# Larger row transfers limited by bytes, a shared phi load, logit blocks by bank pairs, and a moved head order in a convolution and soft-MoE kernel

## The chip, the cores and the metric

The kernel runs on 1 core of one Trainium2 chip. The metric is the device time of one execution in microseconds (us); of several runs the median is taken.

## What is computed

A causal convolution of 7 taps, whose weights are a softmax over the taps of each of 8 heads, is followed by a soft mixture of experts over all 28,672 rows. Everything is float32.

```
x: (8, 3584, 192)   weight: (8 heads, 7 taps)   phi: (192, 32)   w1: (8, 192, 1024)   w2: (8, 1024, 192)
w = softmax(weight, axis=-1)
y[b, s, head h] = sum_k w[h, k] * x[b, s - 6 + k, head h]          # 24 channels a head, zeros before row 0
y = y.reshape(28672, 192)
logits = y @ phi                                                   # (28672, 32 slots)
d = softmax(logits, axis=0); slot_input = d.T @ y                  # over all rows: needs the whole of y
slot_out[e] = relu(slot_input[e] @ w1[e]) @ w2[e]                  # 4 slots for each of 8 experts
out = softmax(logits, axis=1) @ slot_out                           # (28672, 192)
```

## The kernel before

The 8 sequences are 8 batches. A batch's x (2.75 MB) is held in SBUF as 32 windows of 128 rows (`xs`, two buffers in turn), its convolution as `xc` (two buffers), and the transposed convolution as `xt` (one buffer).

- **Loads** (`load_x(b)`): four groups of 8 windows, each in transfers of two windows (256 rows of 768 bytes, 192 KB), and two small transfers for the first window. All DMAs are issued by SyncE (SP), which takes them strictly in order. `load` lets a transfer go only when the one six before it has landed (`WINDOW = 6`). For each group GpSimd (POOL) then copies 6 halo rows (`L184`; for batch 0 in halves, on POOL or ScalarE). The transfers of batch b+2 overwrite `xs` of batch b, so they wait for the last convolution matmul of batch b.
- **Convolution** (`conv(b)`, `L422`): per head 8 matmuls against a banded matrix `toep`, into the PSUM buffers `cv0` and `cv1` in turn, copied to `xc` by ScalarE (ACT, `L182`) or VectorE (DVE, `L186`). Each head reads all of the batch's windows. Batch 0 goes by halves (`L466`). `toep` is built at the start in two halves of four heads, by small copies (`bput`).
- **Transposes** (`turns`, `L443`): six 32x32 block transposes by DVE, one for each block of 32 channels.
- **Logits** (`chain(b)`, `L508`): six blocks k of 32 matmuls, 16 into the bank pair `lg0` (a = 0, 1) and then 16 into `lg1` (a = 2, 3), which accumulate over k. Then a maximum of each bank pair (`fmax`, `L520`, DVE), the running maximum and its negative (`fmin`, `L532` and `L533`), the exponentials (`fexp`, `L539`, ACT, with the negative maximum as bias), eight transposes through the PE (`L554`), their copies, and 64 matmuls that sum the slots' inputs (`L570`), added up in `acc`.
- **The rows' softmax** (`rows(b)`, `L599` to `L619`): maximum, subtraction, exponential, sum and division over the 32 slots, on DVE, POOL and ACT, put into gaps of the schedule.
- **phi**: four DMAs (`L398`) put the same 24 KB on four groups of 32 partitions (`phi4`).
- **Experts and output**: w1 and w2 (12.6 MB) are loaded into gaps and into buffers that come free (`load_w`), the experts run after batch 7 (`L745` to `L799`), then `L828` makes the output, which SP stores (`L850`, `L858`).

The order of all this is written by a planner (`Plan`). Each step is added with a cost for each engine that may run it, what it reads and writes, and a priority (the lower goes first). `Plan.order` simulates the engines with these costs, a delay `LAG` between an engine's end and another's start, and a look-ahead `LOOK`, and emits the steps in the order of the simulated start. Every engine then runs its steps in that order, whatever the real times are. Steps of priority 1000 and above (weights, `rows`) are put into gaps that the first pass left.

Of the kernel before, what the change touches and what calls it, by code (L numbers as in the profile page):

```python
# [10 lines left out]
ALU = mybir.AluOpType  # L11
# [4 lines left out]
class Plan:  # L16
# [2 lines left out]


    ENG = ("PE", "ACT", "DVE", "POOL", "DMA")
    LAG = {"PE": 0.2, "ACT": 0.2, "DVE": 0.16, "POOL": 0.2, "DMA": 2.1}
    SELF = {"PE": 0.0, "ACT": 0.08, "DVE": 0.1, "POOL": 0.1, "DMA": 2.1}
    LOOK = {"PE": 0.05, "ACT": 0.3, "DVE": 0.2, "POOL": 0.0, "DMA": 0.0}
    SLIP = 0.05
# [5 lines left out]
    def add(self, fn, cost, reads=(), writes=(), prio=0.0, after=()):  # L31

        i = len(self.steps)
        deps = {self.writer[r] for r in reads if r in self.writer}
        for w in tuple(writes) + tuple(after):
            if w in self.writer:
                deps.add(self.writer[w])
            deps.update(self.readers.get(w, ()))
        for r in reads:
            self.readers.setdefault(r, []).append(i)  # L40
        for w in writes:
            self.writer[w] = i
            self.readers[w] = []
        deps.discard(i)
        self.steps.append((fn, cost, deps, prio))
# [95 lines left out]
def tile_conv_softmoe(ctx: ExitStack, tc: tile.TileContext, x, weight, phi, w1, w2, out):  # L141
# [12 lines left out]
    TB = T // 2  # L154
    NI = NW // 2
    U = 8
    NB = D // 32
    NQ = S // 4
    TQ = NQ // P
# [8 lines left out]
    def act(n):  # L168
        return 0.19 + n / 1200

    def dve(n):
        return 0.13 + n / 960
# [1 line left out]
    def pool(n):  # L174
        return 0.12 + n * 0.00217

    def dma(nbytes, rate=330e3):
        return {"DMA": nbytes / rate}

    def copy(e, dst, src):  # L180
# [53 lines left out]

    WINDOW = 6
    issued = []

    def load(dst, src):  # L240
        i = nc.sync.dma_start(dst, src).ins  # L241
        if len(issued) >= WINDOW:
            tc.add_manual_dep(
                i, issued[-WINDOW].name, mybir.DependencyInfo(mybir.DependencyClass.Sync, mybir.DependencyReason.DATA),
                reason="short queues",
            )
        issued.append(i)

# [4 lines left out]
    def load_x(b):  # L255
        s = b % 2
        xv = xs[s]
        base = b * S - PRE
        np_ = NW // 4

        def src(row0, rows, i0, n):
            return bass.AP(x.tensor, (base + 2 * T * i0 + row0) * D, ap=[[D, rows], [2 * T * D, n], [1, D]])

        for k in range(4):
            i0, i1 = k * np_, (k + 1) * np_

            def fn(e, k=k, i0=i0, i1=i1):
                if k == 0:

                    nc.sync.dma_start(xv[16:P, 0:1, :], src(16, P - 16, 0, 1))  # L270
                    nc.sync.dma_start(xv[PRE:16, 0:1, :], src(PRE, 16 - PRE, 0, 1))
                    i0 = 1
                if k == 3 and b == B - 1:

                    i1 -= 1
                    nc.sync.dma_start(xv[0:112, i1 : i1 + 1, :], src(0, 112, i1, 1))
                    nc.sync.dma_start(xv[112 : P - 2, i1 : i1 + 1, :], src(112, P - 2 - 112, i1, 1))
                for i in range(i0, i1, 2):
                    n = min(2, i1 - i)
                    load(xv[:, i : i + n, :], src(0, P, i, n))  # L280

            add(fn, dma(P * np_ * D * 4), reads=[f"z{s}"], writes=[xsk[s][k]] + [f"{xsk[s][k]}.{i}" for i in range(2)], prio=b * 10 - 30)

            im = (i0 + i1) // 2
            if b == 0:
                halves = (("POOL", "ACT"), i0, im), (("POOL", "ACT"), im, i1)
            else:
                halves = ((("POOL",), i0, i1),)
            for j, (es, a0, a1) in enumerate(halves):
                add(  # L290
                    lambda e, a0=a0, a1=a1: copy(e, xv[0:ZS, a0:a1, :], xv[64 : 64 + ZS, a0:a1, :]),
                    {en: 0.1 + (a1 - a0) * D * 0.0009 for en in es}, reads=[xsk[s][k]], writes=[f"{xsk[s][k]}.{j}"], prio=b * 10 - 30,
                )

    def load_w(parts, nbytes, key, after, prio):
        def fn(e):
            for dst, src in parts:
                load(dst, src)

        add(fn, dma(nbytes), reads=["begun"], writes=[key], after=after, prio=prio)  # L300

# [1 line left out]
    wv = wb.rearrange("p (h k) -> p h k", k=KT)  # L303
    add(
        lambda e: nc.sync.dma_start(wb, bass.AP(weight.tensor, 0, ap=[[0, P], [1, H * KT]])),
        {"DMA": 0.3}, writes=["wb"], prio=-100,
    )

    add(lambda e: nc.gpsimd.memset(xs[0][0:16, 0, :], 0.0), {"POOL": 0.25}, writes=["z0"], prio=-101)
# [32 lines left out]
    for i in range(2):  # L342
        h0, h1 = i * HG, (i + 1) * HG
        prod = fe[:, (H + h0 * KT) * BW : (H + h1 * KT) * BW].rearrange("p (h c k) -> p h c k", c=BW, k=KT)

        def bprod(e, prod=prod, h0=h0, h1=h1):
            w_ = wv[:, h0:h1, :].unsqueeze(2).broadcast_to((P, HG, BW, KT))
            sh = bass.AP(shf.tensor, shf.offset, ap=[shf.ap[0], [0, HG], [1, BW], [1, KT]])
            veng(e).tensor_tensor(out=prod, in0=sh, in1=w_, op=ALU.mult)

        def bsum(e, prod=prod, h0=h0, h1=h1):
            nc.vector.tensor_reduce(out=band[:, h0:h1, :], in_=prod, axis=AX.X, op=ALU.add)

        n = HG * BW * KT
        add(bprod, {"POOL": pool(n)} if i else {"DVE": dve(n)}, reads=["wb", "shf"], writes=[f"prod{i}", f"e0.{i}"], prio=-42 + i)
        add(bsum, {"DVE": dve(n)}, reads=[f"prod{i}"], writes=[f"band{i}"], prio=-40 + i)


        for a, (p0, rows, off, blks) in enumerate((
            (0, 32, -8 - ZS, (0,)), (0, 8, T - ZS, (1,)), (32, 32, 24 - ZS, (0, 1)),  # L360
            (64, 32, -ZS, (0, 1)), (96, 32, 32 - ZS, (0, 1)),
        )):
            for k in blks:
                t0, t1 = max(TB * k, off), min(TB * k + 32, off + BW)

                def bput(e, p0=p0, rows=rows, off=off, h0=h0, h1=h1, t0=t0, t1=t1, k=k):
                    sl = slice(p0, p0 + rows)
                    copy(e, toep[sl, h0:h1, t0 + (32 - TB) * k : t1 + (32 - TB) * k], band[sl, h0:h1, t0 - off : t1 - off])

                m = HG * (t1 - t0)  # L370
                add(
                    bput, {"ACT": act(m), "DVE": dve(m), "POOL": 0.15 + m * 0.0011}, reads=[f"band{i}", "tz"],
                    writes=[f"toep{i}.{a}.{k}"], prio=-40 + i,
                )
    toepk = [[f"toep{i}.{a}.{k}" for a, k in ((0, 0), (1, 1), (2, 0), (2, 1), (3, 0), (3, 1), (4, 0), (4, 1))] for i in range(2)]
# [18 lines left out]
        )  # L394

    def phi_load(e):
        for a in range(4):
            nc.sync.dma_start(phi4[32 * a : 32 * a + 32], phi.rearrange("(k p) n -> p k n", p=32))  # L398


    def selector(e):
        nc.vector.tensor_reduce(out=gsel[:, 0:NS], in_=ident.rearrange("p (g n) -> p n g", n=NS), axis=AX.X, op=ALU.add)
# [8 lines left out]
    def conv(b):  # L411
# [3 lines left out]
        for h in range(H):  # L415
# [15 lines left out]
                    cv[k][:, :, 0 : NI * CG].rearrange("p f (i c) -> p f i c", c=CG),  # L431
                )

            add(mm, {"PE": 0.72}, reads=all_(xk) + toepk[h // HG], writes=[f"cv{k}"], prio=pr)
            add(ev, {"ACT": act(2 * NI * CG), "DVE": dve(2 * NI * CG)}, reads=[f"cv{k}", "one"], writes=xck[s][h], prio=pr)

    def turns(b):
# [59 lines left out]
    def chain(b):  # L497
# [1 line left out]
        last = b == B - 1  # L499
        n = U * TB  # L500

        for k in range(NB):

            def lmm(e, k=k):
                for a in range(4):
                    r = slice(32 * a, 32 * a + 32)
                    for c in range(4):
                        nc.tensor.matmul(  # L508
                            lg[a // 2][32 * c : 32 * c + 32, a % 2, 0:n].rearrange("p (u j) -> p u j", j=TB),
                            phi4[r, k, :], xt[r, k, U * c : U * c + U, 0:TB],  # L510
                            start=(k == 0), stop=(k == NB - 1), tile_position=(32 * a, 32 * c),
                        )

            add(lmm, {"PE": 0.66}, reads=xtk[k] + ["phi4"], writes=["lg0", "lg1", "lmm"], prio=pr)

        el = eall[:, b].rearrange("p (g u k j) -> p g k u j", g=2, k=2, j=TB)
        for g in range(2):
# [11 lines left out]
        mx, old, nm = nmr[:, b + 1, 2:3], nmr[:, b, 2:3], nmr[:, b, 3:4]  # L529

        def fmin(e):
            nc.vector.tensor_reduce(out=mx, in_=nmr[:, b, 0 : 3 if b else 2], axis=AX.X, op=ALU.max)  # L532
            nc.vector.tensor_scalar(out=nm, in0=mx, scalar1=-1.0, scalar2=None, op0=ALU.mult)  # L533

        add(fmin, {"DVE": 0.2}, reads=[f"nr{b}.{g}" for g in range(2)] + [f"nm{b - 1}"], writes=[f"nm{b}"], prio=pr)
        for g in range(2):

            def fexp(e, g=g):
# [6 lines left out]
        if b:  # L545
            add(
                lambda e: nc.scalar.activation(al[b % 2], old, AF.Exp, bias=nm),
                {"ACT": 0.2}, reads=[f"nm{b}", f"nm{b - 1}"], writes=[f"al{b % 2}"], prio=pr + (0.5 if last else 0),
            )
        for v in range(2):  # L550

# [75 lines left out]
        add(turn, {"DVE": dve(n)}, writes=ks, prio=pr + 100)  # L627

    load_x(0)
    add(phi_load, {"DMA": 0.5}, reads=["xs0.3"], writes=["phi4"], prio=-25)  # L630
    load_x(1)
    conv_halves(0)
    for b in range(B):
# [40 lines left out]
    for i in range(8):  # L674
# [7 lines left out]

    add(
        lambda e: nc.tensor.matmul(cv[0][:, 0, 0:P], mxf.broadcast_to((P, P)), ident, start=True, stop=True),
        {"PE": 0.25}, reads=[f"nm{B - 1}", "ident"], writes=["cv0"], prio=75.5,
    )

    def merge(e):
# [202 lines left out]
```

## Time and profile before

| | |
|---|---|
| median of 3 runs | 227.83 us (226.12 to 228.55) |
| profiled execution | 230.08 us, of which the span from first to last instruction is 228.2 us |
| mean granted TensorE clock of that execution | 0.918 |
| read from HBM and written to it | 37.79 MB and 22.02 MB |

PE is TensorE, PEld its weight loads, SP SyncE's queue. A wait is named by what ended last before it. The profiled execution took 1.0% more than the median.

### The profile page before, as it was taken

Reading aid. Unit: us, or ns where it says so; the run is one execution under the profiler, and the core shown is the slowest. Engines: PE = TensorE matmul, PEld = TensorE weight load, DVE = VectorE, ACT = ScalarE, POOL = GpSimd, SP = SyncE. Lnnn points to the kernel's source line nnn. Section 1 sums busy time; section 2 is a strip of 40 time slices with the busy share of each in tenths; the row PEclk is TensorE's granted clock in tenths of the full one; section 3 lists DMA queues with packets and bytes.
Section 4 is the critical chain, followed back from the end, with each engine's and each line's share of the span. In section 5 each row is a group of like instructions: output and inputs, shape, how many; then the busy total and the mean of one; then the engine's idle time right before and its main releaser. Section 6 shows DMA issues by size and latency. Waiting matters only on the chain.

```text
span 228.2 us, 7982 instructions
## 1 busy us (share of the span) xinstructions
PE 181.1 (79%) x3410; PEld 112.5 (49%) x3410; DVE 155.1 (68%) x236; ACT 91.9 (40%) x140; POOL 100.5 (44%) x110
## 2 busy tenths in 40 slices
PE   4586469989969979999779999989989999776000
PEld 2164335325425525436325546655768899765000
DVE  5999318948759869899649999576277986544000
ACT  3465205456225156173065292322147755456000
POOL 5642556616633585725846624227755850000000
PEclk9999859999979999999979999999999999877555
DMA  4997988789969998486774698889109999999995
GB/s 124 276 283 203 313 253 262 266 254 284 294 196 272 282 266 264 117 247 197 230 201 123 153 206 236 269 280 302 47 28 359 375 404 411 411 413 406 415 417 236
DMA packets 49583, 60.33 MB, mean 264 GB/s; under 512 B 4606, under 2 KB 43404, under 8 KB 49548
## 3 DMA queue, kind: packets, MB, share of 16 engines
q1 hardware_dynamic: 49548, 59.82, 81.0%
q8 instruction: 27, 0.44, 0.8%
q14 instruction: 8, 0.07, 0.1%
HBM read 37.79 MB, written 22.02 MB: 262 GB/s over the span
## 4 chain that ended last, share of the span: by engine, by line
PE 37%; DMA 30%; SPq 8%; DVE 5%; issue 4%; ACT 4%; POOL 4%; DVEq 1%; ACTq 0%; POOLq 0%
DMA xs<-in_x_dram 26%; PE cv L422 10%; PE cv L828 8%; PE lg L570 6%; SPq L241 6%; DMA out_dram<-xt 4%; PE lg L508 2%; PE lg L785 2%; POOL eall L611 2%; PE lg L828 2%; PE lg L554 2%; ACT xs L182 2%; PE cv L745 2%; POOL xs L184 1%; PE cv L676 1%
## 5 line engine op out<-in xcount | busy, mean ns | idle before, releaser
L184 POOL COPY xs<-xs 6x1536 f32<-6x1536 f32 (+1 forms) x31 | 43.3, 1396 | 57.3 <-DMA xs<-in_x_dram 55.1
L422 PE MATMUL cv<-xs,toep 64*64 64x384 f32 x448 | 52.3, 540 | 12.1 <-POOL xs L184 6.3
L182 ACT COPY xc<-cv 128x768 f32<-128x768 f32 x40 | 32.4, 819 | 56.7 <-PE cv L422 53.9
L443 DVE STREAM_TRANSPOSE xt<-xc 128x1024 f32<-128x1024 f32 x42 | 49.1, 1215 | 1.3 <-ACT xc L182 1.3
L508 PE MATMUL lg<-xt,phi 32*32 32x224 f32 x1536 | 32.5, 361 | 4.0 <-issue 2.0
L422 PEld LDWEIGHTS cv<-xs,toep 64*64 64x64 f32 x448 | 16.3, 141 | 37.0 <-issue 11.6
L828 PE MATMUL cv<-so,eall 32*128 32x192 f32 x256 | 30.0, 457 | 4.6 <-ACT xs L182 2.1
L611 POOL TENSOR_TENSOR eall<-eall,rms 128x896 f32<-128x896 f32 x16 | 26.9, 1699 | 14.7 <-DVE rms L615 9.7
L508 PEld LDWEIGHTS lg<-xt,phi 32*32 32x32 f32 x1536 | 19.6, 103 | 19.3 <-issue 10.5
L828 PEld LDWEIGHTS cv<-so,eall 32*128 32x128 f32 x256 | 24.1, 314 | 8.2 <-ACT xs L182 3.3
L186 DVE COPY xc<-cv 128x768 f32<-128x768 f32 x20 | 18.9, 955 | 11.2 <-PE cv L422 10.7
L570 PE MATMUL lg<-xc,dn 128*32 128x193 f32 x512 | 22.8, 329 | 0.3 <-ACT dn L182 0.3
L828 PE MATMUL lg<-so,eall 32*128 32x192 f32 x192 | 22.2, 415 | 0.0
L828 PEld LDWEIGHTS lg<-so,eall 32*128 32x128 f32 x192 | 20.5, 323 | 0.4 <-DVE xs L186 0.2
L619 DVE STREAM_TRANSPOSE eall<-eall 128x896 f32<-128x896 f32 x16 | 17.5, 1099 | 4.0 <-POOL eall L611 4.0
L570 PEld LDWEIGHTS lg<-xc,dn 128*32 128x32 f32 x512 | 15.7, 110 | 8.7 <-ACT dn L182 4.7
L182 ACT COPY xs<-cv 128x768 f32<-128x768 f32 x14 | 11.1, 800 | 16.2 <-PE cv L828 13.8
L539 ACT ACTIVATE dT<-lg,nmr 128x448 f32<-128x448 f32 x16 | 9.3, 632 | 13.4 <-DVE nmr L533 13.3
L602 POOL TENSOR_TENSOR tree<-eall 128x448 f32<-128x448 f32 x8 | 9.2, 1153 | 11.1 <-ACT eall L623 10.9
L186 DVE COPY xs<-cv 128x768 f32<-128x768 f32 x10 | 9.4, 952 | 5.8 <-PE lg L828 2.9
L520 DVE TENSOR_SCALAR_CACHE_REDUCE eall<-lg 128x448 f32<-128x448 f32 x16 | 9.3, 615 | 5.8 <-PE lg L508 5.7
L186 DVE COPY xs<-lg 128x384 f32<-128x384 f32 (+1 forms) x11 | 7.9, 727 | 5.8 <-DMA out_dram<-xs 5.8
(100 smaller groups left out, 191.1 us busy)
## 6 DMA issues: line engine op xcount, KB each, us to landing
xs<-in_x_dram SPq DMA_DIRECT2D x119, 192.0 KB, 4.1
out_dram<-xs SPq DMA_DIRECT2D x20, 672.0 KB, 10.6
out_dram<-xt SPq DMA_DIRECT2D x8, 672.0 KB, 11.5
w1a<-in_moe_w_dram SPq DMA_DIRECT2D x16, 256.0 KB, 5.2
xs<-in_moe_w_dram SPq DMA_DIRECT2D x20, 192.0 KB, 4.3
xt<-in_moe_w_dram SPq DMA_DIRECT2D x12, 192.0 KB, 4.1
out_dram<-xs SPq DMA_DIRECT2D x3, 768.0 KB, 6.0
xs<-in_moe_w_dram SPq DMA_DIRECT2D x8, 256.0 KB, 7.0
```

What stands on the lines that cost most here:

```text
L182: nc.scalar.copy(dst, src)
L184: nc.gpsimd.tensor_copy(dst, src)
L186: nc.vector.tensor_copy(dst, src)
L241: i = nc.sync.dma_start(dst, src).ins
L422: nc.tensor.matmul(cv[k][64 * g : 64 * g + 64, hf, 0 : NI * CG].rearrange("p (c i d) -> p c i d", c=4, d=CG), toep[r, h, :], xv[r, g, :, : ...
L443: nc.vector.transpose(xt[:, k], xc[s][:, :, 1 + 32 * k : 33 + 32 * k])
L508: nc.tensor.matmul(lg[a // 2][32 * c : 32 * c + 32, a % 2, 0:n].rearrange("p (u j) -> p u j", j=TB), phi4[r, k, :], xt[r, k, U * c : U * c ...
L520: nc.vector.tensor_scalar(out=el[:, g], in0=lg[g][:, :, 0:n].rearrange("p k (u j) -> p k u j", j=TB), scalar1=1.0, scalar2=None, op0=ALU.m ...
L570: nc.tensor.matmul(lg[0][32 * c : 32 * c + 32, 1, 0:D1], dn[:, u, 32 * c : 32 * c + 32], xc[s][:, U * c + u, :], start=(u == 0), stop=(u = ...
L611: return lambda e: veng(e).tensor_tensor(out=ev, in0=ev, in1=rb, op=op)
L619: turn = lambda e: nc.vector.transpose(eall[:, b], eall[:, b])
L828: nc.tensor.matmul(banks[c][:, (q - k) * D : (q - k + 1) * D], cb[r, :, q], so[r, :], start=True, stop=True, tile_position=(32 * c, 0),)
```

## The change

Row transfers take half a group (four windows, 384 KB; the group that has the first window, or in batch 7 the last, gives one of three). `load` gets each transfer's bytes and holds a transfer until the earlier ones under way and itself make at most 1.6 MB: four transfers of x, six of w1, eight of w2 (192 KB each). phi is loaded once, and POOL makes the three other copies. The last two logit blocks become two steps: blocks 4 and 5 for `lg0`, then blocks 4 and 5 for `lg1`. For batches 1 to 6 the planner is told that logit block 2 comes after head 1 of the next batch's convolution (`HEADS_AT`, the key `cm{b}.{h}`). The bias of the exponential comes from one reduction with its sign turned; the maximum itself is made afterwards (`fkeep`). POOL no longer makes copies of the first half of `toep`. The planner counts DMAs as slower (315 instead of 330 KB a us, 2.6 instead of 2.1 us of delay; 0.9 us for the taps).

```diff
     ENG = ("PE", "ACT", "DVE", "POOL", "DMA")
-    LAG = {"PE": 0.2, "ACT": 0.2, "DVE": 0.16, "POOL": 0.2, "DMA": 2.1}
+    LAG = {"PE": 0.2, "ACT": 0.2, "DVE": 0.16, "POOL": 0.2, "DMA": 2.6}
     SELF = {"PE": 0.0, "ACT": 0.08, "DVE": 0.1, "POOL": 0.1, "DMA": 2.1}
...
     U = 8
+    HEADS_AT = (2,)
     NB = D // 32
...
-    def dma(nbytes, rate=330e3):
+    def dma(nbytes, rate=315e3):
         return {"DMA": nbytes / rate}
...
-    WINDOW = 6
+    UNDERWAY = 1600000
     issued = []
-    def load(dst, src):
+    def load(dst, src, nbytes):
         i = nc.sync.dma_start(dst, src).ins
-        if len(issued) >= WINDOW:
-            tc.add_manual_dep(
-                i, issued[-WINDOW].name, mybir.DependencyInfo(mybir.DependencyClass.Sync, mybir.DependencyReason.DATA),
-                reason="short queues",
-            )
-        issued.append(i)
+        total = nbytes
+        for earlier, n in reversed(issued):
+            total += n
+            if total > UNDERWAY:
+                tc.add_manual_dep(
+                    i, earlier.name, mybir.DependencyInfo(mybir.DependencyClass.Sync, mybir.DependencyReason.DATA),
+                    reason="short queues",
+                )
+                break
+        issued.append((i, nbytes))
...
                     nc.sync.dma_start(xv[112 : P - 2, i1 : i1 + 1, :], src(112, P - 2 - 112, i1, 1))
-                for i in range(i0, i1, 2):
-                    n = min(2, i1 - i)
-                    load(xv[:, i : i + n, :], src(0, P, i, n))
+                im = (i0 + i1) // 2
+                for a, n in ((i0, im - i0), (im, i1 - im)):
+                    load(xv[:, a : a + n, :], src(0, P, a, n), P * n * D * 4)
...
             for dst, src in parts:
-                load(dst, src)
+                load(dst, src, nbytes // len(parts))
...
         lambda e: nc.sync.dma_start(wb, bass.AP(weight.tensor, 0, ap=[[0, P], [1, H * KT]])),
-        {"DMA": 0.3}, writes=["wb"], prio=-100,
+        {"DMA": 0.9}, writes=["wb"], prio=-100,
     )
...
                 add(
-                    bput, {"ACT": act(m), "DVE": dve(m), "POOL": 0.15 + m * 0.0011}, reads=[f"band{i}", "tz"],
+                    bput, {"ACT": act(m), "DVE": dve(m), **({"POOL": 0.15 + m * 0.0011} if i else {})}, reads=[f"band{i}", "tz"],
                     writes=[f"toep{i}.{a}.{k}"], prio=-40 + i,
...
     def phi_load(e):
-        for a in range(4):
-            nc.sync.dma_start(phi4[32 * a : 32 * a + 32], phi.rearrange("(k p) n -> p k n", p=32))
+        nc.sync.dma_start(phi4[0:32], phi.rearrange("(k p) n -> p k n", p=32))
+    def phi_copies(e):
+        for a in range(1, 4):
+            nc.gpsimd.tensor_copy(phi4[32 * a : 32 * a + 32], phi4[0:32])
...
-            add(mm, {"PE": 0.72}, reads=all_(xk) + toepk[h // HG], writes=[f"cv{k}"], prio=pr)
+            add(mm, {"PE": 0.72}, reads=all_(xk) + toepk[h // HG], writes=[f"cv{k}", f"cm{b}.{h}"], prio=pr)
             add(ev, {"ACT": act(2 * NI * CG), "DVE": dve(2 * NI * CG)}, reads=[f"cv{k}", "one"], writes=xck[s][h], prio=pr)
...
-        for k in range(NB):
-            def lmm(e, k=k):
-                for a in range(4):
-                    r = slice(32 * a, 32 * a + 32)
-                    for c in range(4):
-                        nc.tensor.matmul(
-                            lg[a // 2][32 * c : 32 * c + 32, a % 2, 0:n].rearrange("p (u j) -> p u j", j=TB),
-                            phi4[r, k, :], xt[r, k, U * c : U * c + U, 0:TB],
-                            start=(k == 0), stop=(k == NB - 1), tile_position=(32 * a, 32 * c),
-                        )
-            add(lmm, {"PE": 0.66}, reads=xtk[k] + ["phi4"], writes=["lg0", "lg1", "lmm"], prio=pr)
+        def lstep(ks, gs, deps):
+            def lmm(e):
+                for k in ks:
+                    for a in [2 * g + i for g in gs for i in range(2)]:
+                        r = slice(32 * a, 32 * a + 32)
+                        for c in range(4):
+                            nc.tensor.matmul(
+                                lg[a // 2][32 * c : 32 * c + 32, a % 2, 0:n].rearrange("p (u j) -> p u j", j=TB),
+                                phi4[r, k, :], xt[r, k, U * c : U * c + U, 0:TB],
+                                start=(k == 0), stop=(k == NB - 1), tile_position=(32 * a, 32 * c),
+                            )
+            add(
+                lmm, {"PE": 0.33 * len(ks) * len(gs)}, reads=all_(xtk[k] for k in ks) + ["phi4"] + deps,
+                writes=[f"lg{g}" for g in gs] + ["lmm"], prio=pr,
+            )
+        for k in range(NB - 2):
+            lstep([k], [0, 1], [f"cm{b + 1}.{k // 2}"] if k in HEADS_AT and 0 < b < B - 1 else [])
+        for g in range(2):
+            lstep([NB - 2, NB - 1], [g], [])
...
         def fmin(e):
-            nc.vector.tensor_reduce(out=mx, in_=nmr[:, b, 0 : 3 if b else 2], axis=AX.X, op=ALU.max)
-            nc.vector.tensor_scalar(out=nm, in0=mx, scalar1=-1.0, scalar2=None, op0=ALU.mult)
-        add(fmin, {"DVE": 0.2}, reads=[f"nr{b}.{g}" for g in range(2)] + [f"nm{b - 1}"], writes=[f"nm{b}"], prio=pr)
+            nc.vector.tensor_reduce(out=nm, in_=nmr[:, b, 0 : 3 if b else 2], axis=AX.X, op=ALU.max, negate=True)
+        def fkeep(e):
+            nc.vector.tensor_scalar(out=mx, in0=nm, scalar1=-1.0, scalar2=None, op0=ALU.mult)
+        add(fmin, {"DVE": 0.1}, reads=[f"nr{b}.{g}" for g in range(2)] + [f"mx{b - 1}"], writes=[f"nm{b}"], prio=pr)
+        add(fkeep, {"DVE": 0.1}, reads=[f"nm{b}"], writes=[f"mx{b}"], prio=pr + 1)
         for g in range(2):
...
                 lambda e: nc.scalar.activation(al[b % 2], old, AF.Exp, bias=nm),
-                {"ACT": 0.2}, reads=[f"nm{b}", f"nm{b - 1}"], writes=[f"al{b % 2}"], prio=pr + (0.5 if last else 0),
+                {"ACT": 0.2}, reads=[f"nm{b}", f"mx{b - 1}"], writes=[f"al{b % 2}"], prio=pr + (0.5 if last else 0),
             )
...
     load_x(0)
-    add(phi_load, {"DMA": 0.5}, reads=["xs0.3"], writes=["phi4"], prio=-25)
+    add(phi_load, {"DMA": 0.45}, reads=["xs0.3"], writes=["phi4"], prio=-25)
+    add(phi_copies, {"POOL": 0.9}, writes=["phi4"], prio=-15)
     load_x(1)
...
         lambda e: nc.tensor.matmul(cv[0][:, 0, 0:P], mxf.broadcast_to((P, P)), ident, start=True, stop=True),
-        {"PE": 0.25}, reads=[f"nm{B - 1}", "ident"], writes=["cv0"], prio=75.5,
+        {"PE": 0.25}, reads=[f"mx{B - 1}", "ident"], writes=["cv0"], prio=75.5,
     )
```

## Rows read from the trace of the kernel before

**Rows 1.** The page, busy time of each engine over the whole span

```profile
PE 181.1 (79%) x3410; PEld 112.5 (49%) x3410; DVE 155.1 (68%) x236; ACT 91.9 (40%) x140; POOL 100.5 (44%) x110
```

**Rows 2.** Windows of 10 us: PE, PEld, DVE, ACT, POOL, clock, DMA share, GB/s

```profile
80.00:90.00 10.00, 8.75 (x144) 4.29 (x148) 8.25 (x13) 6.45 (x10) 7.34 (x5) 1.00 0.97 286
90.00:100.00 10.00, 9.72 (x256) 4.41 (x248) 8.71 (x16) 3.05 (x5) 4.54 (x7) 1.00 0.52 149
...
110.00:120.00 10.00, 7.03 (x96) 2.48 (x78) 5.31 (x11) 3.97 (x7) 6.79 (x5) 0.83 0.77 219
...
210.00:220.00 10.00, 0.12 (x2) 0.00 (x0) 1.20 (x2) 0.51 (x2) 0.00 (x0) 0.56 1.01 413
```

**Rows 3.** Who waited for whom: us in total, times, longest

```profile
POOL xs L184 <- DMA xs<-in_x_dram: 55.1, 28, 6.3
```

**Rows 4.** Timeline of the start: start, us, engine, line, what, count, idle before

```profile
14.71 1.89 SPq L398 DMA_DIRECT2D phi<-in_moe_phi_dram  x4
...
21.50 3.71 PE L508 MATMUL lg<-xt,phi 32*32 32x224 f32 x188 [1.48 <-DVE xt L490]
23.05 1.46 POOL L184 COPY xs<-xs 6x1536 f32<-6x1536 f32 x1 [3.23 <-DMA xs<-in_x_dram]
...
29.22 1.46 POOL L184 COPY xs<-xs 6x1536 f32<-6x1536 f32 x1 [2.29 <-DMA xs<-in_x_dram]
```

**Rows 5.** Timeline of PE, batches 0 to 5

```profile
30.73 3.10 PE L422 MATMUL cv<-xs,toep 64*64 64x384 f32 x16 [5.52 <-POOL xs L184]
...
56.42 1.52 PE L422 MATMUL cv<-xs,toep 64*64 64x384 f32 x16
57.87 3.12 PE L508 MATMUL lg<-xt,phi 32*32 32x224 f32 x160
...
64.49 1.00 PE L508 MATMUL lg<-xt,phi 32*32 32x224 f32 x16 [2.01 <-issue]
...
79.92 1.08 PE L422 MATMUL cv<-xs,toep 64*64 64x384 f32 x8 [0.42 <-POOL xs L184]
...
85.18 0.88 PE L422 MATMUL cv<-xs,toep 64*64 64x384 f32 x8 [0.97 <-DVE xc L186]
...
110.58 1.08 PE L422 MATMUL cv<-xs,toep 64*64 64x384 f32 x8 [0.35 <-POOL xs L184]
...
115.70 3.85 PE L422 MATMUL cv<-xs,toep 64*64 64x384 f32 x24 [2.62 <-ACT xc L182]
```

**Rows 6.** Timeline of all engines around the load of batch 6, and at the end of batch 7

```profile
92.18 0.33 SPq L270 DMA_DIRECT2D xs<-in_x_dram  x1
...
109.07 1.46 POOL L184 COPY xs<-xs 6x1536 f32<-6x1536 f32 x1 [2.63 <-DMA xs<-in_x_dram]
...
113.99 0.95 ACT L623 ACTIVATE eall<-eall 128x896 f32<-128x896 f32 x1 [6.57 <-POOL eall L611]
...
145.40 0.15 DVE L533 TENSOR_SCALAR nmr<-nmr 128x1 f32<-128x1 f32 x1
145.67 1.16 ACT L539 ACTIVATE dT<-lg,nmr 128x448 f32<-128x448 f32 x2 [5.54 <-DVE nmr L533]
```

**Rows 7.** The chain that ended last, batch 6's load: start, us, what

```profile
93.37 1.58 SPq L241
...
95.50 4.77 DMA xs<-in_x_dram
```

**Rows 8.** SP's load instructions: ns least/median/most, first and last start

```profile
L241 SPq DMA_DIRECT2D xs<-in_x_dram x128: 346/413/2506, 2.0 to 120.2; - x128
...
L241 SPq DMA_DIRECT2D w1a<-in_moe_w_dram x16: 327/334/1077, 36.8 to 75.6; - x16
```

**Rows 9.** Windows of 1 us, in the columns of rows 2

```profile
19.00:20.00 1.00, 0.64 (x6) 0.14 (x4) 1.00 (x2) 1.00 (x2) 0.82 (x1) 1.00 0.47 111
...
24.00:25.00 1.00, 1.00 (x65) 0.70 (x50) 0.00 (x0) 0.00 (x0) 0.51 (x1) 1.00 1.04 348
...
99.00:100.00 1.00, 0.72 (x12) 0.21 (x8) 0.96 (x3) 0.90 (x3) 0.00 (x0) 1.00 0.64 204
```

## The prediction, made before the kernel ran

> **What bounds the kernel now.** I read the page first: no engine is full over the span, PE leads with 79% [rows 1]. So I went on to windows of 10 us [rows 2], and they show two halves. From 170 us on the DMA engines are full at some 410 GB/s, which is the storing of 22 MB; nothing in the change touches that, and whatever the first half gains moves it as a whole. In the first half DVE and PE are busy 8 to 9 tenths and the DMA share swings between 0.97 and 0.52 while x is being loaded. A resource that is at half while others wait for it is limited by how it is fed. The view of waits says who waits: the halo copies stand 55.1 us for x, far ahead of anything else [rows 3].
>
> Then I followed one load, batch 6's [rows 6]. SP issues it from 92.18 us; the last halo copy starts at 109.07 and ends at 110.53. That is 18.4 us for 2.75 MB, of which 9.6 would do at the 286 GB/s that 80 to 90 us shows [rows 2]. The chain has the reason: one issue took 1.58 us and the transfer issued at 95.50 landed 4.77 us later [rows 7], while in 99 to 100 us the DMA engines are 0.64 busy at 204 GB/s [rows 9]. An issue of 192 KB takes 0.41 us in the median and up to 2.51 [rows 8]; with two issues a microsecond SP feeds some 390 GB/s, so after a slow one it refills its six transfers hardly faster than the DMA engines empty them. Where nothing disturbed it the same window of six kept them full: share 1.04, 348 GB/s [rows 9]. So the descriptors (768 bytes, which don't change) are not the limit at 204 GB/s; the refill is.
>
> What a late load costs on PE: 5.52 us before batch 1's convolution, 0.42 before batch 4's, and 2.62 at 113 to 115.7 [rows 5]. The last looks like ACT's fault. It is the load's: the halo copy at 109.07 holds POOL, the row step `L611` comes after it, ACT's exponential `L623` stands 6.57 us for that [rows 6], and the evacuation that PE needs is behind it on ACT.
>
> **The change, part by part.** All terms are in the profiled execution (230.08 us, of which 228.2 are span; 1.0% above the median).
>
> *Transfers of 384 KB, 1.6 MB under way.* Per batch 8 large issues replace 16, and 1.57 MB are under way where it was 1.18. The trace has no issue of 512 rows. Per instruction it lies between that of 128 descriptors (0.33 us, the w1 rows) and twice that of 256 (0.83) [rows 8]; at the upper end SP gains nothing per byte. I take 0.55, nearer the lower, since 128 to 256 descriptors added only 0.08. Refilling then goes at some 700 KB a us, twice what the engines take, and a slow issue of 1.5 us is covered by what is still queued (1.18 MB, the three transfers behind the one that is awaited, are 3.4 us at 348 GB/s). A load should come to 9.6 us, about 3 for the first transfer's way and 1.46 for the halo: 14 us, or 3 to 4 less than batch 6's. Queued behind a waiting issue on SP are only other loads, here w1's, which have slack.
>
> At the start: phi's four issues take SP from 14.71 to 16.60 [rows 4], and the DMA share falls to 0.47 at 19 us [rows 9]. One issue gives back about 1.4 us, the faster refill some more. Batch 1's convolution, which PE waits 5.52 us for, comes 2.0 us sooner: **-2.0** (-0.5 to -4.0).
>
> The POOL, ACT and PE queue-up at 113 us goes if the halo is 3 us earlier: 2.62, and what follows at half clock, where 24 matmuls take 3.85 us against 2.28 by the 1.52 for 16 [rows 5], together 4.2. I take **-3.5** (0 to -4.2), since the planner will draw a new order. Of the clock: the granted clock of that stretch is 0.83 of 2.4 GHz [rows 2], that is, 1.2 GHz for a third of it, and PE had stood idle just before. The Trainium skill (TensorE: Matmul & The Clock Gate, section "Loop structure matters more than you think") says that PE runs cold after a long wait for a DMA. By it the 1.57 us go with the wait; if the clock fell for another cause, the sum would be -4.6 in place of -6.2.
>
> The 2.01 us at 62.5 [rows 5] are put down to nothing the profile shows, so I count 0 (0 to -2.0).
>
> *phi's three copies.* POOL takes them: the halo row of 6x1536 costs 1.46 us, so 192 elements lie between 0.2 and 0.8 each; I take 0.35, 1.05 in all. Behind them on POOL are batch 1's halo copies. The cover is POOL's own wait of 3.23 us before 23.05 [rows 4]. phi is needed whole by 21.50, when the logits of batch 0 begin in earnest; if DMA and copies end later than that, they cost what exceeds it, but PE would wait for x afterwards anyway. 0.
>
> *The first half of `toep` without POOL*: DVE or ACT makes copies more, at worst about 1 us on DVE before batch 0's logits end at 25.21 [rows 4]. Cover: PE's wait until 30.73, of which 2 us go. 0.
>
> *Two heads ahead of logit block 2.* PE runs blocks 0 to 4 of batch b now while x of b+1 lands (3.12 us for five [rows 5]). Afterwards it wants heads 0 and 1 when two are done, 1.87 us sooner, and blocks 2 to 5 are queued behind the wait. Where the load is ready this moves nothing in sum: the same matmuls. Where it isn't, up to 1.87 us a batch stand open. Batches 4 and 6 make PE wait for the halo already now (0.42 and 0.35 us [rows 5]), and I count a third that may come just in time, so up to 3 x 1.87 = 5.6. With loads 3 us faster two of the three are in time; batch 4, whose load goes behind six w1 transfers, is the doubtful one. **+0.8** (-0.4, batch 4's present wait gone, to +5.6). What it brings: the heads' copies are made under the logits, so that PE waits less for them between logits and exponentials. Six such waits, the longest 0.97 [rows 5], come to 2.6: **-1.2** (0 to -2.6).
>
> *Bank pairs and the bias in one operation.* In batches 1 to 6 heads fill the time between. In batch 7 it is open: one DVE operation of 0.15 us and its gap leave the path to the exponential [rows 6]. With pairs the first maximum runs beside the second pair's matmuls, which gains up to 0.6 if PE came last, nothing if DVE's transposes did (then both pairs wait for them). **-0.3** (0 to -0.8). `fkeep` adds 0.15 us to DVE off the path.
>
> *The planner's costs* only redraw the order; no row prices that. It is why I take less than the full size above.
>
> Sum: -2.0 -3.5 +0.8 -1.2 -0.3 = -6.2 of 230.08, 2.7%; from the median **221.7 us**.
>
> **The rivals.** *The loads don't get faster.* For it: 80 to 90 us reached 286 GB/s with the old transfers [rows 2], so where SP isn't disturbed there is little to gain, and a double issue time would leave SP's rate as it was. Against: 99 to 100 us. PE would then wait as now and the redrawn order would give the two heads' time back among evacuations; what stays is phi's issues and the tail, -1.0 -0.3: 226.5. The Trainium skill (DMA: Bandwidth & Descriptors, "Anatomy of one DMA") would have it so: it fits a DMA (issued by another engine) with 2.0 us plus bytes at 436 GB/s. By that, as an estimate, six transfers of 192 KB carry 1.18 MB in 2.45 us, 481 GB/s, more than the engines move, so size and count would gain nothing. The window of 348 GB/s agrees, that of 204 doesn't.
>
> *The heads in front cost more than the loads give (slower).* Its place is PE's queue before logit block 2, its price 1.87 us in each batch whose x is late, three of them or more; it decides as soon as loads shorten by less than that. For it: w1's transfers go ahead of x on the same queue, and more of their bytes are under way in front of batch 4's first. With 4 to 5 us lost and nothing at the start: 232.
>
> *All of it comes*: the ends of all gains, -4.0 -2.0 -4.2 -0.4 -2.6 -0.8 = -14: 214, PE then being full through the first half. Against: DVE is at 8 to 9 tenths too.
>
> **How the numbers follow.** Forecast 0.54 (217.5 to 225.5 is its own range), no faster loads 0.20, slower 0.16, all of it 0.10. A measurement of this kernel can't tell less than about 1% from no change, here 2.3 us. Faster: 0.54 + 0.10 = 0.64; within 1%: 0.20; slower: 0.16. The range 217 to 230 holds the forecast, the first rival, and the near edges of the other two, which leaves out some 0.2.
>
> **What the profile of the changed kernel would show.** Right: batch 1's convolution starts near 28.7; the last halo copy of a batch ends 14 to 15 us after its first issue; DMA share above 0.85 wherever x is loaded; no wait of more than 1 us of PE for ACT after 100 us. Wrong: issues of 0.8 us or more; PE waiting for POOL's halo copies in several batches with logits behind it; a chain through SP's issues and x as long as now. The prediction fails most easily by a redrawn order that puts some row step in front of an evacuation again.

## The result and the profile after

The changed kernel takes 218.44 us in the median of six runs (217.78 to 222.99), the kernel before 228.97 in runs beside it: 0.9583 of its time, with a 95% interval of 0.9516 to 0.9650. It is faster, as forecast, and by more: 4.2% where I had 2.7%. The span of the profiled execution is 216.6 us, where it was 228.2. Ratios here and below leave out executions more than 1.5% above the fastest of the same kernel, which are slow whatever the kernel, and so 218.44 over 228.97 does not give 0.9583.

Windows of 10 us of the changed kernel, in the columns of rows 2:

```profile
80.00:90.00 10.00, 9.07 (x268) 5.30 (x258) 7.47 (x14) 1.88 (x3) 6.58 (x8) 1.00 0.65 192
90.00:100.00 10.00, 9.71 (x185) 5.19 (x184) 9.42 (x11) 5.25 (x10) 6.64 (x6) 1.00 0.54 158
...
110.00:120.00 10.00, 9.25 (x266) 5.13 (x256) 6.45 (x10) 2.26 (x3) 7.35 (x8) 1.00 0.58 140
...
200.00:210.00 10.00, 0.00 (x0) 0.00 (x0) 0.00 (x0) 0.00 (x0) 0.00 (x0) 0.50 1.02 415
```

PE is 9 tenths busy or more in the three stretches of the first half shown here, and at full clock; the one from 110 us had 7.03 and a granted clock of 0.83 [rows 2]. The DMA share is low there now for another reason: the loads are over early and wait for the next buffer. In windows of 1 us, batch 6's load (first issue at 82.26) has a share of 0.37 to 0.89 from 83 to 87 us, then 1.02 to 1.11 until 94, and 0.13 or less from 95 to 98; the next load is issued at 97.83, when the convolution matmuls that read its buffer have ended at 97.75. The store at the end runs at 415 GB/s (413 before).

Who waited for x, and the timeline of PE (start, us, what, idle before), of the changed kernel:

```profile
POOL xs L185 <- DMA xs<-in_x_dram: 38.9, 26, 3.4
```

```profile
21.08 5.30 PE L516 MATMUL lg<-xt,phi 32*32 32x224 f32 x188 [1.78 <-DVE xt L497]
...
26.79 1.72 PE L429 MATMUL cv<-xs,toep 64*64 64x384 f32 x16 [0.41 <-POOL xs L185]
...
54.10 1.72 PE L429 MATMUL cv<-xs,toep 64*64 64x384 f32 x16 [1.05 <-POOL xs L185]
...
84.44 1.73 PE L429 MATMUL cv<-xs,toep 64*64 64x384 f32 x16 [0.93 <-POOL xs L185]
...
114.17 1.62 PE L429 MATMUL cv<-xs,toep 64*64 64x384 f32 x16 [0.71 <-POOL xs L185]
...
122.34 0.88 PE L429 MATMUL cv<-xs,toep 64*64 64x384 f32 x8 [1.23 <-DVE xc L187]
```

Batch 1's convolution starts at 26.79 instead of 30.73, and its first 16 matmuls take 1.72 us instead of 3.10 [rows 5]: the granted clock is 1.00 from 26.7 to 28.5 us, where it was 0.53 from 30.7 to 33.85, which is close to 1.2 GHz. The slow clock is not gone, it comes earlier: batch 0's logits take 5.30 us instead of 3.71 [rows 4], at 0.50 from 24 to 25 us. It costs nothing visible there, since they end at 26.38 and the halo copy that PE needs next only at 26.73. In f1, another execution of the changed kernel (below), the slow clock is back at its old place, behind a wait of 3.09 us (in f3 too, behind 2.02 us):

```profile
27.55 3.04 PE L429 MATMUL cv<-xs,toep 64*64 64x384 f32 x16 [3.09 <-POOL xs L185]
```

The waits of 2.01 and 2.62 us are not in the changed kernel's first trace. New are waits for the halo before the two heads that were moved forward, 1.05 us at most, and one of 1.23 us for DVE in batch 7's convolution.

The start of the slots' transposes (`L554`, `L573` after) marks each batch on PE's timeline; in us:

| batch | 0 | 1 | 2 | 3 | 4 | 5 | 6 | 7 |
|---|---|---|---|---|---|---|---|---|
| before | 33.76 | 51.82 | 70.06 | 85.98 | 101.06 | 119.48 | 133.77 | 147.37 |
| changed | 28.58 | 46.26 | 61.88 | 76.70 | 92.27 | 106.65 | 123.15 | 135.03 |
| earlier by | 5.2 | 5.6 | 8.2 | 9.3 | 8.8 | 12.8 | 10.6 | 12.3 |

So 5.2 us came at the start, 2.6 between batches 1 and 2, 4.0 between 4 and 5; 2.2 were given back between 5 and 6, where the waits of 0.71 and 1.23 us stand, and 1.7 came again at the end. The other steps are 1.1 us or less. What follows (the experts, the output) moves along but for 0.7: the span is 11.6 us shorter. These are steps of single traces, and two executions of one kernel can differ by as much: e1 and f2 below are one kernel, and its batch 0 stands at 32.65 in one trace and at 28.79 in the other.

### The profile page after: what moved, and what is told of

It reads as the page before. It is cut to its first block, busy times and chain, and to the rows that moved or that the text cites. A ratio compares the mean times of both kernels' runs of the same rounds, so it can differ in the third digit from the quotient of the medians.

```text
span 216.6 us, 7865 instructions
## 1 busy us (share of the span) xinstructions
PE 178.4 (82%) x3410; PEld 116.5 (54%) x3410; DVE 154.4 (71%) x232; ACT 92.8 (43%) x146; POOL 102.7 (47%) x111
## 4 chain that ended last, share of the span: by engine, by line
DMA 37%; PE 35%; POOL 6%; DVE 5%; SPq 3%; issue 3%; ACT 2%; DVEq 1%; POOLq 0%; ACTq 0%
DMA xs<-in_x_dram 31%; PE cv L429 7%; PE cv L848 6%; PE lg L589 5%; PE lg L516 5%; DMA out_dram<-xs 4%; PE lg L848 3%; PE lg L805 2%; DMA w1a<-in_moe_w_dram 2%; POOL xs L185 2%; SPq L242 2%; PE lg L573 2%; PE cv L765 2%; POOL eall L630 2%; PE cv L696 1%
## 5 line engine op out<-in xcount | busy, mean ns | idle before, releaser
L185 POOL COPY xs<-xs 6x1536 f32<-6x1536 f32 (+1 forms) x32 | 44.1, 1380 | 40.5 <-DMA xs<-in_x_dram 38.9
L450 DVE STREAM_TRANSPOSE xt<-xc 128x1024 f32<-128x1024 f32 x42 | 50.4, 1227 | 3.4 <-ACT xc L183 2.7
L429 PE MATMUL cv<-xs,toep 64*64 64x384 f32 x448 | 46.6, 501 | 6.5 <-POOL xs L185 3.4
L516 PE MATMUL lg<-xt,phi 32*32 32x224 f32 x1536 | 34.8, 372 | 2.1 <-DVE xt L497 1.8
L848 PE MATMUL cv<-so,eall 32*128 32x192 f32 x256 | 28.9, 470 | 5.2 <-ACT xs L183 2.3
L516 PEld LDWEIGHTS lg<-xt,phi 32*32 32x32 f32 x1536 | 24.1, 105 | 15.1 <-issue 4.8
L429 PEld LDWEIGHTS cv<-xs,toep 64*64 64x64 f32 x448 | 15.4, 131 | 27.2 <-ACT xc L183 6.8
L848 PEld LDWEIGHTS cv<-so,eall 32*128 32x128 f32 x256 | 22.8, 316 | 9.0 <-ACT xs L183 3.9
L183 ACT COPY xs<-cv 128x768 f32<-128x768 f32 x15 | 11.9, 801 | 16.1 <-PE cv L848 14.4
L625 POOL TENSOR_TENSOR tree<-tree 128x224 f32<-128x224 f32 (+2 forms) x24 | 10.9, 454 | 1.9
```

The costliest lines, as they stand in the source:

```text
L183: nc.scalar.copy(dst, src)
L185: nc.gpsimd.tensor_copy(dst, src)
L429: nc.tensor.matmul(cv[k][64 * g : 64 * g + 64, hf, 0 : NI * CG].rearrange("p (c i d) -> p c i d", c=4, d=CG), toep[r, h, :], xv[r, g, :, : ...
L450: nc.vector.transpose(xt[:, k], xc[s][:, :, 1 + 32 * k : 33 + 32 * k])
L516: nc.tensor.matmul(lg[a // 2][32 * c : 32 * c + 32, a % 2, 0:n].rearrange("p (u j) -> p u j", j=TB), phi4[r, k, :], xt[r, k, U * c : U * c ...
L625: nc.gpsimd.tensor_tensor(out=dst, in0=tree[:, :, 0:w], in1=tree[:, :, w : 2 * w], op=op)
```

## The experiments

Whether loads or order carried it was open, and both parts are large. The planner's costs don't depend on the size of a transfer, so the loads could be exchanged with the order on PE, DVE, ACT and POOL left exactly as it is. Below, "bytes behind" is what the limit leaves queued behind the transfer that SP waits for.

**The new loads alone** (e1), in the kernel before:

```diff
-    WINDOW = 6
+    UNDERWAY = 1600000        # and load() with bytes, as in the change
-                for i in range(i0, i1, 2): ...
+                for a, n in ((i0, im - i0), (im, i1 - im)): ...
```

> The kernel before with the transfers of 384 KB and the limit of 1.6 MB alone; the order on PE, DVE, ACT and POOL is the one of before. If the loads carry most of the gain (my prediction's view), it comes to 220 to 223 us against 228. If the redrawn order carries it (heads ahead of logit block 2, new planner costs), it stays within 226 to 228.5.

Measured: 0.9583 of before (0.9507 to 0.9659), the changed kernel's own ratio; the median of 219.95 us lies just under the range expected. The loads alone bring it all, as far as intervals of 0.7 to 0.8% each way can tell. From batch 4's transposes to batch 5's it takes 15.2 us in its trace instead of 18.4, in the order of before.

**The old loads in the new order** (e2), the reverse:

> The changed kernel with the old loads (192 KB, six under way), the new order kept. Loads carry the gain: 226 us or more, since two heads stand in front of the logits and meet late rows (my slower rival would even give 230 to 232). Order carries it: 219 to 221.

Measured: 0.9893 (0.9835 to 0.9951), a median of 228.03 us, as expected if the loads carry the gain. Everything but the loads (the order, phi, the bank pairs, the bias) is worth 1.1%. The kernel isn't slower, but the wait that my slower rival named is there. PE's timeline of this kernel:

```profile
61.00 1.73 PE L429 MATMUL cv<-xs,toep 64*64 64x384 f32 x16 [2.57 <-POOL xs L185]
...
77.44 1.73 PE L429 MATMUL cv<-xs,toep 64*64 64x384 f32 x16 [1.88 <-POOL xs L185]
...
94.74 1.72 PE L429 MATMUL cv<-xs,toep 64*64 64x384 f32 x16 [2.51 <-POOL xs L185]
...
125.08 1.73 PE L429 MATMUL cv<-xs,toep 64*64 64x384 f32 x16 [1.31 <-POOL xs L185]
```

These four are 8.3 us of waiting in front of heads 0 and 1, more than I priced (at most 5.6). That the kernel is still not slower says that the rest of the change gives back at least as much elsewhere: the wait of 2.62 us for ACT, for one, isn't in it, and from batch 4's transposes to batch 5's it takes 14.5 us.

**Small transfers, more of them** (e3), **large transfers, fewer** (e4): the changed kernel with

```diff
# e3: transfers of two windows (192 KB), 1.6 MB under way
-                for a, n in ((i0, im - i0), (im, i1 - im)):
-                    load(xv[:, a : a + n, :], src(0, P, a, n), P * n * D * 4)
+                for i in range(i0, i1, 2):
+                    n = min(2, i1 - i)
+                    load(xv[:, i : i + n, :], src(0, P, i, n), P * n * D * 4)
# e4: transfers of four windows (384 KB)
-    UNDERWAY = 1600000
+    UNDERWAY = 1200000
```

> The changed kernel with transfers of 192 KB, but eight of them (1.57 MB) under way; order kept. If SP's refill by issue count is the limit, it loses much of the loads' gain: 222 to 226 us. If the bytes under way are what counts, it stays at 218 to 220.

> The changed kernel with transfers of 384 KB, but only 1.2 MB under way (three; w1 four, w2 six); order kept. If issue count is what counts, it stays at 218 to 220 us. If the bytes under way count, it loses: 222 to 226.

Measured: e3 0.9817 (0.9742 to 0.9893), e4 1.0145 (1.0039 to 1.0250). Neither half of the edit does it. e2 is the kernel to compare with, since it has the same order: with 1.18 MB under way as there, large transfers are 2.5% slower than e2 (233.34 us, beyond the range expected) and slower than the kernel before; with small transfers the larger limit brings 0.8%, and the intervals overlap. Both together bring 3.1% against e2. The limit counts w1 and w2 as well, and no run takes their transfers apart from those of x.

SP's load instructions (ns least/median/most), one line each of the changed kernel, e3, e4 and f4 (below):

```profile
L242 SPq DMA_DIRECT2D xs<-in_x_dram x64: 367/368/1305, 2.0 to 106.7; - x64
```

```profile
L242 SPq DMA_DIRECT2D xs<-in_x_dram x128: 347/467/2682, 2.0 to 117.1; - x128
```

```profile
L242 SPq DMA_DIRECT2D xs<-in_x_dram x64: 367/368/2006, 2.0 to 121.8; - x64
```

```profile
L242 SPq DMA_DIRECT2D xs<-in_x_dram x64: 368/507/2791, 2.0 to 112.7; - x64
```

An issue of 512 rows takes no longer (0.368 us) than one of 256 (0.413 [rows 8]). So per byte SP is twice as fast, in e4 too; and e4 is slow all the same. SP's refill by issue count, which I had put first, is not enough. What orders e4, e2 and the changed kernel is the bytes behind: two transfers (0.79 MB) 1.0145, five of 192 KB (0.98 MB) 0.9893, three of 384 KB (1.18 MB) 0.9583. e3 has 1.38 MB behind and doesn't fit this line; there SP's issues take 0.467 us in the median, for half the bytes. The loads of these four kernels, which share one order, do stand in the order of the times: from the first issue to the end of the last halo copy it takes, in the mean of batches 1 to 7, 17.8 us in e4, 17.5 in e2, 17.2 in e3 and 16.3 in the changed kernel (18.2 before, 16.4 in e1). With e1 and e2 that shows that the loads set the time. That a load needs both, enough bytes behind and few issues, is how I read these four runs; what holds up an issue in e3 isn't shown.

**Beside the changed kernel on one chip** (f1): the loads alone again (f2), the order of heads undone (f3), more bytes (f4):

```diff
# f3
-    HEADS_AT = (2,)
+    HEADS_AT = ()
# f4
-    UNDERWAY = 1600000
+    UNDERWAY = 2400000
```

> The changed kernel again, beside the next three on one chip. 0.958 of the kernel before.

> The kernel before with the new loads alone, again. If the other parts (phi, heads, pairs, bias, planner) bring something on top of the loads, it is 1 to 1.5% slower than the changed kernel (3 us at the start and the tail, as its trace shows batch 1's halo 3 us later). If what they bring is given back by the heads' waits, the two are within 0.7%.

> The changed kernel without the order 'block 2 after head 1'. In the changed kernel PE waits for POOL's halo copies before the moved heads in batches 2, 3, 5 and 7 (0.31 to 1.05 us each, some 3.0 in all). If the moved heads cost that and give nothing, this kernel is 1 to 1.5% faster than the changed one. If what they give (evacuations under the logits) is as large, the two are within 0.7%; if larger, it is slower.

> The changed kernel with up to 2.4 MB under way (six transfers of 384 KB). If the bytes under way still limit, a further 1 to 2%. If four transfers cover SP's slow issues, no change within 0.7%.

Measured: f1 0.9574 (0.9513 to 0.9636); f2 a median of 220.92 us (216.50 to 222.34) against f1's 219.57 (217.09 to 222.11), too wide for a ratio of its own but no slower in its best run; f3 0.9586 (0.9537 to 0.9635); f4 0.9692 (0.9637 to 0.9747). So the moved heads neither cost nor give anything that can be told, once the loads are in time. And 2.4 MB are worse, by 1.2% against f1, with intervals that just part; I had expected a gain or no change. There 20 of SP's 82 issues of x take over 1 us, against one in the changed kernel. Yet f4's rows of batches 3 to 7 arrive as fast as those of the changed kernel (14.8 to 16.1 us from the first issue to the last halo). Against f1's trace it loses 1.8 us between batches 1 and 2 (19.5 against 17.7 us), where PE stands still in batch 2's logits. First f4, then f2:

```profile
59.02 2.36 PE L516 MATMUL lg<-xt,phi 32*32 32x224 f32 x106
63.41 0.95 PE L516 MATMUL lg<-xt,phi 32*32 32x224 f32 x22 [2.04 <-issue]
```

```profile
58.51 0.60 PE L508 MATMUL lg<-xt,phi 32*32 32x224 f32 x13 [2.34 <-issue]
```

That is the wait that stood at the same place before (2.01 us [rows 5]). It isn't f4's own: besides f2, the traces of g1 (1.96 us), g4 (1.76), g3 (1.15) and f1 (0.94) have it there. The changed kernel's first trace and e1 have none, and they are the same kernels as f1 and f2. So it comes and goes between executions of one kernel, whatever the limit. Its cause stays open, and so does that of f4's 1.2%.

**The rest, part by part** (all in the changed kernel): phi by four loads (g1), the planner's old DMA costs and POOL in `bput` (g2), six logit blocks over both bank pairs with the bias in two operations (g3), 2.0 MB under way (g4):

```diff
# g1 (and no phi_copies); everything else stays in the same order
-        nc.sync.dma_start(phi4[0:32], phi.rearrange("(k p) n -> p k n", p=32))
+        for a in range(4): nc.sync.dma_start(phi4[32 * a : 32 * a + 32], phi.rearrange("(k p) n -> p k n", p=32))
# g2
-    LAG = {..., "DMA": 2.6}    rate=315e3    {"DMA": 0.9}
+    LAG = {..., "DMA": 2.1}    rate=330e3    {"DMA": 0.3}    # and POOL again in bput
# g3
-        for k in range(NB - 2): ...
-        for g in range(2):
-            lstep([NB - 2, NB - 1], [g], [])
+        for k in range(NB): ...       # and fmin with two operations
# g4
+    UNDERWAY = 2000000
```

> The changed kernel with phi by four loads again and no copies by POOL; everything else in the same order. If phi's three extra issues hold up batch 1's rows as I costed (about 1.4 us of the 2.0 at the start), batch 1's halo ends 1 to 1.5 us later and the kernel is 0.4 to 0.6% slower, at the edge of what can be told. If SP's other slack hides them, no difference.

> The changed kernel with the planner's old DMA costs (2.1 us, 330 KB a us, 0.3 us for the taps) and POOL allowed for the first half of toep. If the redrawn order is worth what the mixed parts hide, 1% slower than the changed kernel. If order matters little once the loads are in time: within 0.7%.

> The changed kernel with six logit blocks over both bank pairs and the bias in two operations, as before. From the traces, the time from the end of batch 7's logits to the transposes falls from 3.4 to 2.5 us by these two; so 0.9 us at the end of the first half should come back, 0.4%. If they also shorten the six batches before, more than 1%.

> The changed kernel with 2.0 MB under way (five transfers of 384 KB); order kept. If the optimum lies between four and six, equal or up to 0.5% faster than the changed kernel. If SP's issues already block at five (in the run with 2.4 MB 20 of 82 issues took over 1 us), 0.3 to 1% slower.

Measured: g1 0.9595 (0.9533 to 0.9656), g2 0.9588 (0.9542 to 0.9635), g3 0.9596 (0.9520 to 0.9671), g4 0.9592 (0.9527 to 0.9658). All four agree with the changed kernel (0.9583 and 0.9574); none of these parts is worth as much as intervals of 0.5 to 0.8% each way can tell, and the 0.4 to 0.6% expected of g1 and g3 would be hidden in them. Three things can be read from the traces instead.

phi's four issues are no shorter in g1 than before (1.89 us [rows 4]). Its timeline, SP and POOL:

```profile
12.52 2.34 SPq L402 DMA_DIRECT2D phi<-in_moe_phi_dram  x4
...
14.95 6.23 SPq L242 DMA_DIRECT2D xs<-in_x_dram  x6
...
25.62 1.46 POOL L185 COPY xs<-xs 6x1536 f32<-6x1536 f32 x1 [0.84 <-DMA xs<-in_x_dram]
```

They hold SP for 2.34 us, and batch 1's last halo copy ends at 27.08, where it ended at 26.73 with one issue. That is 0.35 us instead of the 1 to 1.5 expected. f2, with four issues and the order of before, starts batch 1's convolution at 26.90.

The end of batch 7's logits, PE's timeline of the changed kernel and of g3:

```profile
128.55 3.94 PE L516 MATMUL lg<-xt,phi 32*32 32x224 f32 x192
...
135.03 1.04 PE L573 MATMUL lg<-ident,dT 128*128 128x128 f32 x8
```

```profile
128.72 4.42 PE L516 MATMUL lg<-xt,phi 32*32 32x224 f32 x192
...
137.07 1.04 PE L568 MATMUL lg<-ident,dT 128*128 128x128 f32 x8
```

From the logits' end (start and duration added: 132.49 and 133.14) to the transposes it is 2.54 us with the pairs and 3.93 without them. That is 1.4 us in these two traces, of which 0.80 is a wait in g3 that its profile puts down to nothing. To the first exponential it is 0.98 us (133.47) with the pairs and the bias in one operation, and 1.52 (134.66) without; 1.72 before (145.67 [rows 6], logits' end 143.95).

And g4, with 1.57 MB behind, has 5 issues over 1 us: nothing gained over 1.18 MB. Four transfers are enough here.

## Why the prediction was right, step by step

*The loads are limited by how they are fed, and PE waits for them.* Right, and shown: e1 and e2. From the first issue to the last halo copy, batches 3 to 7 took 16.9 to 20.6 us before and take 15.6 to 16.5 now. I had expected 14: the 3 us for the first transfer's way came from no row, and in batch 6's load the DMA engines are full only from 87 us, 4.7 us after the first issue. My reading of the share of 0.52 from 90 to 100 us was too strong: from 91 to 92 us it is 0.03 and from 92 to 93 it is 0.00, since the next load is only issued at 92.18. The rest of that stretch is as I read it (0.23 at 95 us, 0.64 at 99). Of the two reasons I gave, the share of refill by fewer issues was overrated: e4 has it and is slower than the kernel before. The cover by what is queued behind, which I named second, is what e4, e2 and the changed kernel are ordered by, and e3 shows that it isn't enough by itself.

*The start, -2.0.* The term that was mis-sized: 30.73 to 26.79 is 3.9 us, at the far end of my -0.5 to -4.0, and 1.4 more come from the clock, which I had counted in the queue-up at 113 us and forgotten here: the same 16 matmuls at full clock. Together 5.2 us by the transposes of batch 0. How much of it the change brings isn't settled: f1, the same kernel, has the slow clock there again and gains 3.2 us (30.52), and the loads alone gain 1.1 in e1 and 5.0 in f2. And my reason was half wrong: of phi's 1.4 us, g1 shows 0.35.

*The queue-up of POOL, ACT and PE, -3.5.* Between batches 4 and 5 it is 4.0 us less, and PE's wait of 2.62 us and the half clock are gone. Earlier loads alone do that (e1, 3.2 us less), and so does the rest of the change with late loads (e2, 4.0 less). The granted clock is 1.00 from 30 us until 160 us in the windows of 10 us, so the 1.57 us went with the wait. This stage agrees with the Trainium skill's sentence on waits for DMAs (TensorE: Matmul & The Clock Gate, section "Loop structure matters more than you think"). Other stages show that a wait does not tell by itself: in e2 the wait of 2.57 us is followed by a granted clock of 1.00 (61.0 to 62.7 us), in g2 one of 1.55 us by 0.58 (54.8 to 57.8).

*0 for the 2.01 us at 62.5.* It stands. 2.6 us went between batches 1 and 2 in the changed kernel's first trace, but the wait comes and goes between executions of one kernel (none and 0.94 us in the changed kernel, none and 2.34 in that of e1), so that its absence there is luck and no gain that the runs show.

*The heads, +0.8 and -1.2.* In sum nothing, as f3 has it (0.9586 against 0.9574). The waits for the halo are there (3.0 us over four before moved heads in the changed kernel, 8.3 over four in e2), though not in batch 4, which I had called the doubtful one. So the price of the slower rival was real; its error was to count that price against the kernel before, as if the rest gave nothing. With the old loads the rest of the change is 1.1% faster in spite of it.

*The tail, -0.3.* It was 3.42 us before, is 2.54 now: -0.9, just past the end of -0.8.

*phi, `toep` and the planner, 0.* Right within what can be told (g1, g2).

*The first rival, loads that get no faster*, falls with e1. By my estimate from the Trainium skill's fit (DMA: Bandwidth & Descriptors, "Anatomy of one DMA") six transfers of 192 KB were enough; e1 against the kernel before speaks against carrying that over to a stream that SP feeds under a limit. *All of it*, 214, was nearer than I held likely.

*The signs.* No wait of PE for ACT is longer than 0.29 us after 100 us, and batch 1's convolution starts even before 28.7. The DMA share is above 0.85 only in the middle of batch 6's load. One sign of being wrong came true, PE waiting for halo copies before moved heads in four batches, and the time was right all the same.

## What to carry to other kernels

In a stream of transfers under a limit, count the bytes queued behind the one that is awaited, and not only the transfers or the bytes in all: making the pieces larger under the same limit takes them away (e4). They are not the whole of it: small pieces with more behind did worse (e3), and beyond 1.18 MB behind nothing more came (g4, f4). Where a stretch of the profile shows full DMA engines and the next one half empty ones with the same descriptors, see first whether a load was under way at all, and then look at the issuing queue before the transfers. Before a step of a single trace is put down to a change, look for it in a second execution of the same kernel. And when the part that feeds everything is mended, fine reordering around it may no longer be worth anything that can be measured: here everything but the loads gave 1.1% with the old loads, and nothing that could be told beside the new ones.

## What the runs showed of the hardware that was not expected

- An issue of 512 rows of 768 bytes takes SP 0.368 us in the median, one of 256 rows 0.413 to 0.467. The median does not grow with the rows.
- With 2.4 MB under way SP's own issues take longer: 0.507 us in the median for 512 rows and up to 2.79, and 20 of 82 over 1 us, against one of 82 at 1.6 MB and 5 at 2.0.
- The limit of 1.2 MB with 384 KB transfers is 5.9% slower than that of 1.6 MB (1.0145 against 0.9583 of the kernel before), for one transfer less under way.
- The slow clock at the start moves between executions: batch 0's logits take 5.30 us in the changed kernel's first trace and 3.91 in f1, and batch 1's first 16 matmuls 1.72 and 3.04.
